# A Fourier mixing layer and a two-layer MLP in one kernel: the first MLP layer's blocks by seven products instead of eight

## The chip, the core and the metric

The kernel runs on one core of a Trainium2 chip. A core has a matrix engine (TensorE, PE in the profile; PEld is its load of the stationary operand), a vector engine (DVE), an activation engine (ACT), a general engine (POOL) and a queue for transfers (SP). Each engine works through its own list of instructions in order, and waits between engines are semaphores. Matmul results go to PSUM banks (tiles named `d`), from which ACT and DVE read them. The metric is the device time of a run in microseconds; lower is better.

## The reference

```python
h  = x + irfft2(rfft2(layernorm(x)) * (w_r + 1j * w_i))     # x: 2048 tokens x 576
h2 = h + relu(layernorm(h) @ w1) @ w2                        # w1: 576 x 4608, w2: 4608 x 576
```

All data is float32. The change concerns the last line only.

## The kernel before

The first part of the kernel computes the Fourier part by matmuls with constant tables. Then the normalised tokens lie transposed in four tiles `xc[c]` of 512 tokens each, and the MLP runs over 18 groups of 256 hidden units (`NG`), and in each group over the 4 token blocks. The sum over groups stays in `xs` (tile A) in SBUF.

**Three matmuls for a product.** TensorE is fed with the type float32r. To keep float32's precision, each operand is held as a high part `h` (ACT copies the value into float32r) and a low part `l` (the value minus `h`, on DVE or POOL); that pair of instructions is `split`. A product is then three matmuls: `h*h`, `h*l` and `l*h`.

**Layer 1.** `mm1` multiplies 128 hidden units by 512 tokens over a depth of 576: four tiles of 128 with three matmuls each, and a last tile of 64 that holds high and low side by side and takes two. That is 14 matmuls of 512 columns, and 28 for the 256 units of a step.

**Layer 2.** In groups 0 and 1 `mm2` does it plainly. From group 2 on (`WINO = 8`, the ninth step), the block of 256 units by 512 tokens and the block of `w2` are each cut into 2 by 2 parts, and the four part products come from seven products instead of eight (Winograd's form of Strassen's method): `prod` does one, with six matmuls of 288 columns, in one of two PSUM banks in turn. It needs sums and differences of the hidden parts (S1 to S4: POOL, then `split`) and of the weights (T1 to T4). After each product `add` (DVE, 128 x 576) adds the bank's present state to `xs`, and the next product but one goes into the same bank.

**The order.** Every engine's list is written by hand: it is the order of the calls in the code. `slot(i)` does layer 2 of step i while it does layer 1 of step i + 1, in four quarters: seven matmuls of layer 1, then two products of layer 2 with their adds, and between them the reading of the hidden block (`hid_a`: `relu_split` and a `Relu` copy), the splits and the next group's weights. The 64th slot, `slot_last`, has no layer 1 beside it and takes eight plain products.

Of the kernel before, what the change touches and what calls it, by code (L numbers as in the profile page):

```python
# [128 lines left out]
def kernel(ctx: ExitStack, tc: tile.TileContext, x, w_r, w_i, w1, w2, cc2, c1, fb, ib, c3, out):  # L129
    nc = tc.nc  # L130
    pool = ctx.enter_context(tc.tile_pool(name="sb", bufs=1))
    psum = ctx.enter_context(tc.tile_pool(name="ps", bufs=1, space=PSUM))

# [172 lines left out]
    def load_weights(g):  # L306
        v1, v2 = ebuf([128, 5, 256]), ebuf([128, 2, D])
# [4 lines left out]
        nc.sync.dma_start(v2, w2[f, :].rearrange("(a p) d -> p a d", p=128))  # L312
        raw[g] = (v1, v2)
# [4 lines left out]

    pieces = []

    def work(k):
        for _ in range(k):
            split(*pieces.pop(0))

    def split_weights(g, part):
# [6 lines left out]
        for k in range((5, 2)[part]) if g >= 2 else [slice(None)]:  # L332
            pieces.append((h[:, k], l[:, k], raw[g][part][:, k]))
        if g <= 2:
            work(len(pieces))
# [79 lines left out]
    xs = sb([128, NT, D], "A")  # L415
# [106 lines left out]
    hid = {}  # L522
    pend = {}

    def mm1(i, a, part=None):
        g, c = steps[i]
        w1h, w1l = wts[g, 0]
        if a == 0 and not part:
            pend[i] = None if i >= WINO else ps()
        p = hid_p(i, a) if i >= WINO else pend[i][:, 512 * a:512 * a + 512]  # L530
# [5 lines left out]
        for n_, (w, kt, xk) in enumerate(ops):  # L536
            if part is None or n_ // 7 == part:
                mm(p, w[:, kt, f], xc[c][:, xk, :], n_ == 0, n_ == len(ops) - 1)
        if i >= WINO:
            return  # L540
        if a == GF - 1:
            p = pend.pop(i).rearrange("p (a s) -> p a s", a=GF)
            hh, hl = sb([128, GF, 512], "D", 4, F32R), sb([128, GF, 512], "D", 4, F32R)
            nc.scalar.activation(hh, p, AF.Relu)  # L544
            nc.vector.scalar_tensor_tensor(hl, p, 0.0, hh, op0=ALU.max, op1=ALU.subtract)  # L545
            hid[i] = (hh, hl)

    seen = [0] * NC

    def mm2(i, tt):  # L550
# [12 lines left out]
        if tt == CH - 1:  # L563
            seen[c] += 1
            hid.pop(i)


    WINO = 8
    wps, fs = [], {}
    NAMES = ("B22", "T4", "B11", "B21", "T2", "T1", "T3")  # L570

    def wform(n):
        o = 6208 + 576 * NAMES.index(n)
        return tail[0][:, o:o + 288], tail[0][:, o + 288:o + 576]

    def wino_sums(g, *ns):
        v = raw[g][1]
        if 1 in ns:
            T = ebuf([128, 4, 288])
            fs["T1"], fs["T2"], fs["T3"], fs["T4"] = (T[:, i] for i in range(4))  # L580
            fs["B11"], fs["B12"], fs["B21"], fs["B22"] = v[:, 0, :288], v[:, 0, 288:], v[:, 1, :288], v[:, 1, 288:]
        for n_ in ns:
            o, a, b = (("T1", "B12", "B11"), ("T2", "B22", "T1"), ("T3", "B22", "B12"), ("T4", "B21", "T2"))[n_ - 1]
            nc.gpsimd.tensor_sub(fs[o], fs[a], fs[b])

    def wino_w(*names):
        for n in names:
            split(*wform(n), fs[n])

    def wino_tiles():  # L590
        D1, D2, D3 = (sb([128, 4, 256], "D", 4, F32R) for _ in range(3))
        E1, E2 = ebuf([128, 4, 256]), ebuf([128, 4, 256])
        hs = tail[0][:, 5184:5696], tail[0][:, 5696:6208]
        fs.update(p0=E1[:, 0:2], p1=E1[:, 2:4], S1=E2[:, 0], S2=E2[:, 1], S3=E2[:, 2], S4=E2[:, 3], S12=E2[:, 0:2])
        fs.update(A11=(D1[:, 0], D1[:, 1]), A12=(D1[:, 2], D1[:, 3]), A22=(D2[:, 0], D2[:, 1]), S4f=(D2[:, 2], D2[:, 3]))
        fs.update(S12f=(D3[:, 0:2], D3[:, 2:4]), S1f=(D3[:, 0], D3[:, 2]), S2f=(D3[:, 1], D3[:, 3]))
        fs.update(S3f=(tail[0][:, 5696:5952], tail[0][:, 5952:6208]))
# [6 lines left out]
    def hid_p(i, k):  # L604
        return wps[2 + k][:, 512 * (i % 2):512 * (i % 2) + 512]

    def hid_a(i, k):
        p = hid_p(i, k)
        if k == 0:
            relu_split(fs["A11"], p[:, :256])  # L610
            nc.scalar.activation(fs["p0"], p.rearrange("p (a n) -> p a n", a=2), AF.Relu)  # L611
            nc.gpsimd.tensor_sub(fs["S3"], fs["p0"][:, 0], fs["p0"][:, 1])  # L612
        else:
            relu_split(fs["A12"], p[:, :256])
            nc.scalar.activation(fs["p1"], p.rearrange("p (a n) -> p a n", a=2), AF.Relu)  # L615
            nc.gpsimd.tensor_add(fs["S1"], fs["p0"][:, 1], fs["p1"][:, 1])  # L616
            nc.gpsimd.tensor_sub(fs["S2"], fs["S1"], fs["p0"][:, 0])  # L617
            nc.gpsimd.tensor_sub(fs["S4"], fs["p1"][:, 0], fs["S2"])

    def prod(i, a, b, bank, first, end=True, whole=True):  # L620
        ah, al = fs[a]
        bh, bl = fs["B12f"] if b == "B12" else wform(b)
# [6 lines left out]
    def add(i, bank, *to):  # L629
        c = steps[i][1]  # L630
        P = wps[bank].rearrange("p (a n) -> p a n", a=2)[:, :, :288]
        for hs, hd in to:
            xt = xs[:, CH * c + 2 * hs:CH * c + 2 * hs + 2, 288 * hd:288 * hd + 288]
            nc.vector.tensor_add(xt, xt, P)  # L634
# [20 lines left out]
    def slot(i):  # L655
# [17 lines left out]
        if new:  # L673
            wino_w("T3", "B22")
# [140 lines left out]
```

## Time and profile before

| | |
|---|---|
| median of 3 runs | 1029.68 us (1028.57 to 1029.93) |
| profiled execution, first to last instruction (span) | 1026.5 us |
| median minus that span | 3.2 us |
| PE busy | 1011.1 us (98%) |
| PEld busy | 899.2 us (88%) |
| DVE busy | 741.4 us (72%) |
| ACT busy | 391.1 us (38%) |
| POOL busy | 326.0 us (32%) |
| mean granted clock of TensorE | 0.993 |
| steps 3 to 7, before the first slot | 200.4 to 264.1 us |
| slots | 264.1 to 1014.6 us |
| last block and the last stores | 1014.6 to 1026.5 us |

The profile gives no time of the profiled execution other than its span; the 3.2 us are what the runs' median has beside it. A row of the groups names the source line, the engine, the operation, the tiles written and read, their shape and count, and then the busy time, the mean duration of one, and the idle time of the engine just before them with what ended it. The means include the pipeline's length: neighbours on one engine can start before the one ahead has ended. Line 149 is the helper that issues the matmuls of layer 1 and of `mm2`, 627 the one of the seven products, 634 their adds, 317 the low part of a split, 152 ACT's copy, 584 and 612 to 618 POOL's sums.

### The profile page before, as it was taken

The page shows a single profiled execution, that of the slowest core. Times are in us where ns is not written, and L with a number is a line of the kernel's source. Part 1 is how long each engine was busy: PE and PEld are TensorE (multiplying, and loading weights), DVE is VectorE, ACT ScalarE, POOL GpSimd, SP SyncE. Part 2 cuts the span into 40 slices and gives each one's busy share as a digit, 9 for nine tenths or more (in the row PEclk, how much of TensorE's full clock was granted, in tenths as well). Part 3 has the DMA queues.
Part 4 walks back from the last instruction along what each step waited for, and adds up shares of the span by engine and source line. Part 5 has one row for each costly group of instructions (what it writes and reads, how often), then busy time and mean ns, then how long its engine had stood idle before and what let it go on. Part 6 is the DMA issues. An engine that isn't in the chain of part 4 may idle for free.

```text
span 1026.5 us, 17863 instructions
## 1 busy us (share of the span) xinstructions
PE 1011.1 (98%) x6894; PEld 899.2 (88%) x6894; DVE 741.4 (72%) x1366; ACT 391.1 (38%) x891; POOL 326.0 (32%) x429
## 2 busy tenths in 40 slices
PE   7999999999999999999999999999999999999997
PEld 6877678899999999999999999999999999999997
DVE  7689877334678777777777777877777777777774
ACT  5645354311233343343334343334334333334331
POOL 4201465110233333323232433333332323243321
PEclk7999999999999999999999999999999999999999
DMA  9944500110000000000110000000000011000024
GB/s 243 219 129 115 121 21 30 49 38 13 27 24 27 25 27 24 27 24 27 33 41 27 24 27 24 27 24 26 24 27 24 26 33 41 27 24 1 1 59 127
DMA packets 32101, 48.01 MB, mean 47 GB/s; under 512 B 2960, under 2 KB 22800, under 8 KB 32016
## 3 DMA queue, kind: packets, MB, share of 16 engines
q1 hardware_dynamic: 31280, 45.98, 16.7%
q8 instruction: 55, 0.90, 0.4%
q10 hardware_dynamic: 736, 0.89, 0.3%
q14 instruction: 30, 0.25, 0.1%
HBM read 42.13 MB, written 4.72 MB: 46 GB/s over the span
## 4 chain that ended last, share of the span: by engine, by line
PE 94%; DVE 3%; DMA 2%; SPq 0%; ACT 0%; issue 0%; DVEq 0%; ACTq 0%
PE d L149 58%; PE d L627 35%; DMA A<-in_A_x_dram 2%; DVE st L209 1%; PE d L509 1%; DMA X<-in_A_x_dram 0%; DVE A L469 0%; DVE D L545 0%; DVE e L253 0%; DVE mv L210 0%; ACT D L544 0%; DVE e L252 0%; DVE e L488 0%; SPq L424 0%; SPq L160 0%
## 5 line engine op out<-in xcount | busy, mean ns | idle before, releaser
L634 DVE TENSOR_TENSOR A<-A,d 128x576 f32<-128x576 f32 x445 | 332.5, 747 | 51.2 <-PE d L627 51.0
L627 PE MATMUL d<-X,D 128*128 128x288 f32 x2286 | 342.8, 294 | 0.0
L627 PEld LDWEIGHTS d<-X,D 128*128 128x128 f32 x2286 | 326.4, 188 | 14.7
L149 PE MATMUL d<-B,e 128*128 128x512 f32 x952 | 237.4, 390 | 0.0
L149 PEld LDWEIGHTS d<-B,e 128*128 128x128 f32 x952 | 171.9, 188 | 27.9 <-issue 0.2
L602 DVE SCALAR_TENSOR_TENSOR D<-d,D 128x256 fp32r<-128x256 f32 x191 | 81.1, 425 | 121.8 <-ACT D L601 121.8
L601 ACT ACTIVATE D<-d 128x256 fp32r<-128x256 f32 x191 | 73.0, 382 | 242.3 <-PE d L149 242.3
L616 POOL TENSOR_TENSOR e<-e 128x256 f32<-128x256 f32 x63 | 46.6, 740 | 350.0 <-ACT e L615 350.0
L149 PE MATMUL d<-C,e 128*128 128x512 f32 x476 | 119.0, 390 | 0.0
L149 PE MATMUL d<-X,e 128*128 128x512 f32 x476 | 118.8, 390 | 0.0
L152 ACT ACTIVATE X<-e 128x288 fp32r<-128x288 f32 (+2 forms) x176 | 69.8, 434 | 103.5 <-PE d L627 103.5
L317 DVE TENSOR_TENSOR D<-e,D 128x512 fp32r<-128x512 f32 x126 | 91.2, 724 | 19.5 <-ACT D L152 19.5
L612 POOL TENSOR_TENSOR e<-e 128x256 f32<-128x256 f32 x63 | 46.8, 744 | 170.1 <-ACT e L611 170.1
L149 PEld LDWEIGHTS d<-C,e 128*128 128x128 f32 x476 | 85.9, 188 | 13.8
L149 PEld LDWEIGHTS d<-X,e 128*128 128x128 f32 x476 | 85.9, 188 | 13.7
L152 ACT ACTIVATE D<-e 128x512 fp32r<-128x512 f32 x126 | 65.6, 521 | 73.7 <-POOL e L617 70.2
L317 DVE TENSOR_TENSOR X<-e,X 128x288 fp32r<-128x288 f32 (+2 forms) x176 | 82.8, 493 | 0.3 <-POOL r L212 0.3
L627 PEld LDWEIGHTS d<-X 128*128 128x128 f32 x378 | 57.2, 188 | 4.9
L627 PE MATMUL d<-X 128*128 128x288 f32 x378 | 60.4, 295 | 0.0
L149 PE MATMUL d<-e,D 128*128 128x288 f32 x384 | 52.7, 296 | 0.0
L149 PEld LDWEIGHTS d<-e,D 128*128 128x128 f32 x384 | 51.9, 189 | 0.7 <-ACT e L152 0.2
L617 POOL TENSOR_TENSOR e<-e,e 128x256 f32<-128x256 f32 x63 | 49.7, 790 | 4.9
(86 smaller groups left out, 938.0 us busy)
## 6 DMA issues: line engine op xcount, KB each, us to landing
e<-in_B_w_dram SPq DMA_DIRECT2D x18, 576.0 KB, 4.0
e<-in_B_w_dram SPq DMA_DIRECT2D x18, 512.0 KB, 3.7
A<-in_A_x_dram SPq DMA_DIRECT2D x16, 288.0 KB, 8.7
out_dram<-A SPq DMA_DIRECT2D x28, 144.0 KB, 2.5
X<-in_A_x_dram SPq DMA_DIRECT2D x12, 288.0 KB, 7.4
e<-in_B_w_dram SPq DMA_DIRECT2D x36, 64.0 KB, 3.5
B<-in_A_w_r_dram SPq DMA_DIRECT2D x15, 144.5 KB, 7.5
B<-in_A_w_i_dram SPq DMA_DIRECT2D x15, 144.5 KB, 7.1
```

Of the source, the lines that this page charges most:

```text
L149: nc.tensor.matmul(o, l, r, start=start, stop=stop)
L152: nc.scalar.activation(o, i, AF.Copy, **kw)
L209: nc.vector.bn_stats(st[:, i, h, :], xs[:, t0 + i, 288 * h:288 * h + 288])
L317: eng.tensor_sub(l, v, h)
L509: nc.tensor.transpose(pz[:, 128 * b:128 * b + 128], y[:, 128 * b:128 * b + 128], ident)
L601: nc.scalar.activation(h, p, AF.Relu)
L602: nc.vector.scalar_tensor_tensor(l, p, 0.0, h, op0=ALU.max, op1=ALU.subtract)
L612: nc.gpsimd.tensor_sub(fs["S3"], fs["p0"][:, 0], fs["p0"][:, 1])
L616: nc.gpsimd.tensor_add(fs["S1"], fs["p0"][:, 1], fs["p1"][:, 1])
L617: nc.gpsimd.tensor_sub(fs["S2"], fs["S1"], fs["p0"][:, 0])
L627: nc.tensor.matmul(P[:, tt], l[:, q], r, start=first and n_ == 0, stop=end and n_ == 2, skip_group_check=whole and not first)
L634: nc.vector.tensor_add(xt, xt, P)
```

## The change

From group 2 on, layer 1 is done by seven products too. Its block is 256 units by 1024 tokens, a *double*: two token blocks 2p and 2p + 1. The weights are cut into 2 by 2 parts of 128 units and a depth of 256, the tokens into parts of a depth of 256 and 512 tokens; the last 64 of the depth are added by two plain matmuls at four of the products. The sums of the token parts (T1 to T4, each with high and low part) are the same for every group. They are computed once, in steps 3 to 6 (`sum_jobs`), written to DRAM, and read back when p changes (`load_sum`): T1 and T2 over parts of `xc` that layer 1 no longer needs, T3 and T4 into a tile F. The order of the first eight steps has changed a little, and the scratch for software DMA is smaller.

A double's seven products go to three banks: a (which alternates between two places from double to double), b and c. Bank a collects products 0, 1, 3 and 6, and its state has to be read between them: `p1` after product 0, `u2` after 1, `c2` after 3. The two hidden blocks of the double, Z (second token block) and Y (first), arise from these states (`l1_post`, `l1_late`), with a sum of four POOL instructions for each (`hsum`, into one shared tile). `slot(d)` has seven rounds: in round r, product r of layer 1 of double d + 1, then products 2r and 2r + 1 of layer 2 of double d, then the reading for Y of double d (`l1_late`) and for double d + 1 (`l1_post`), then the weights. There are 31 such slots after the start, and a last one with 15 products of layer 2. Step 7 holds layer 1 of the first double.

```diff
-        for k in range((5, 2)[part]) if g >= 2 else [slice(None)]:
-            pieces.append((h[:, k], l[:, k], raw[g][part][:, k]))
...
+        split(h, l, raw[g][part])
...
+    steps = [(0, 0), (0, 1), (0, 2), (1, 1), (1, 0), (0, 3), (1, 3), (1, 2)]
...
+    def sum_jobs(p):
...
+        def tail_of(name, f, st):
+            h, l = (v3(v) for v in st)
+            jobs.append(lambda: act(h, f))
+            def low():
+                nc.vector.tensor_sub(l, f, h)
+                td[p, name] = d = dram.tile([128, 2, 1024], F32, name=f"t{p}{name}")
+                for k in range(2):
+                    nc.sync.dma_start(d[:, k], st[k].bitcast(F32))
+            jobs.append(low)
+        def diff(f, st, x, y):
+            w = v3(st[1].bitcast(F32))
+            jobs.append(lambda: (nc.gpsimd.tensor_sub(w, x[1], y[1]), nc.vector.tensor_sub(f, x[0], y[0])))
+            jobs.append(lambda: nc.vector.tensor_add(f, f, w))
...
+    def load_sum(p, n):
+        h, l = TF[n]
+        for k, o in enumerate((h, l)):
+            nc.sync.dma_start(o.bitcast(F32), td[p, n][:, k].rearrange("p (a n) -> p a n", a=2))
...
+    def l1_bank(d, n_):
+        k = {"a": d % 2, "b": 2, "c": 3}[n_]
+        return wps[2 + k // 2][:, 512 * (k % 2):512 * (k % 2) + 512]
+    def l1_prod(d, r):
...
+        bank, w, x, first, rest = (("a", "A11", "B11", 1, None), ("a", "S2", "T2", 0, None), ("c", "S1", "T1", 1, (1, 1)), ("a", "S3", "T3", 0, None),
+                                   ("b", "A12", "B21", 1, (0, 0)), ("c", "S4", "B22", 0, (2, 1)), ("a", "A22", "T4", 0, (1, 0)))[r]
+        o = l1_bank(d, bank)
+        (wh, wl), (xh, xl) = W1[w], X[x]
+        ops = [(a[:, k], b[:, k]) for k in range(2) for a, b in ((wh, xh), (wh, xl), (wl, xh))]
...
+    def hsum(p0, p1, o):
+        s1, s2, s3, s4 = (sums[:, 256 * k:256 * k + 256] for k in range(4))
+        nc.gpsimd.tensor_add(s1, p0[:, 256:], p1[:, 256:])
+        nc.gpsimd.tensor_sub(s2, s1, p0[:, :256])
+        nc.gpsimd.tensor_sub(s3, p0[:, :256], p0[:, 256:])
+        nc.gpsimd.tensor_sub(s4, p1[:, :256], s2)
+    def l1_post(d, r):
...
+        if r == 0:
+            act(p1, a)
+        elif r == 1:
+            act(u2, a)
+        elif r == 3:
+            act(c2, a)
+            nc.vector.tensor_add(c2, c2, c)
+            relu(c2, c2)
+            split(*Z["A2"], c2)
+        elif r == 4:
+            nc.vector.tensor_add(p1, p1, b)
+            relu(p1, p1)
+            if 0 < d < LAST:
+                split(*Y["A11"], p1[:, :256])
+        elif r == 5:
+            nc.vector.tensor_add(u2, u2, c)
+            relu(u2, u2)
+            hsum(u2, c2, None)
+            split(*Z["A11"], u2[:, :256])
+        elif r == 6:
+            split(*Z["S12"], sums[:, :512])
+            split(*Z["S34"], sums[:, 512:])
...
+    def l1_late(d, r):
...
+        if r == 0:
+            relu_split(Y["A2"], a)
+            if d < LAST:
+                relu(c2, a)
+                hsum(p1, c2, None)
+        elif d < LAST:
+            if r == 1:
+                split(*Y["S12"], sums[:, :512])
+            elif r == 2:
+                split(*Y["S34"], sums[:, 512:])
...
+    def weights(d, r):
...
+        if turn:
+            if r == 0 and g + 2 < NG:
+                load_w1(g + 2, vs[1])
...
+            if r == 6:
+                w2_split("T34", nc.vector)
+                w2_split("B22", nc.gpsimd)
+            for n_, k in (("T2", 1), ("T1", 2), ("T3", 3), ("T4", 6)):
+                if k == r:
+                    load_sum(doubles[d + 2][1], n_)
+        else:
...
+            if r == 5:
+                w1_split("S34", nc.gpsimd)
+            if r == 6:
+                for n_ in ("A2", "W4", "wd"):
+                    w1_split(n_, nc.gpsimd)
+    def slot(d):
+        for r in range(7):
+            l1_prod(d + 1, r)
+            for m in (2 * r, 2 * r + 1):
+                second(d, m)
+            l1_late(d, r)
+            l1_post(d + 1, r)
+            weights(d, r)
...
+        while jobs:
+            jobs.pop(0)()
+        w2_split("T34", nc.gpsimd)
+        w1_sums()
+        for n_ in ("A11", "S12", "S34", "A2", "W4", "wd"):
+            w1_split(n_, nc.gpsimd)
+        load_w1(FIRST + 1, vs[1])
...
+        for n_ in ("T2", "T1", "T3", "T4"):
+            load_sum(doubles[0][1], n_)
...
+        for r in range(7):
+            l1_prod(0, r)
+            if r % 2:
+                mm2(i, r // 2)
+            l1_post(0, r)
...
-    nc = _bacc.Bacc("TRN2", target_bir_lowering=False, num_devices=1)
+    nc = _bacc.Bacc("TRN2", target_bir_lowering=False, num_devices=1, dynamic_dma_scratch_size=512)
```

Where the instructions stand now, in the lists that the engines follow (line, operation, tile written and read, shape; the numbers behind the letters tell buffers apart).

ACT before, within two slots: L601 and L611 or L615 read a layer-1 bank `d`, D_2728 and X_2063 are high parts of S4 and S3, e_6684 of weights.

```order
L601 ACTIVATE D_2727<-d_2725 128x256
L611 ACTIVATE e_2730<-d_2725 128x512
L152 ACTIVATE D_2728<-e_2731 128x256
L152 ACTIVATE e_6684<-e_6474 128x256
L152 ACTIVATE X_2063<-e_2731 128x256
L601 ACTIVATE D_2727<-d_2726 128x256
L615 ACTIVATE e_2730<-d_2726 128x512
```

ACT now, from round 5 of a slot to round 0 of the next: L566 are relus (the first makes `u2`), A_1376 is `hsum`'s tile (D_2807 takes Z's S12, X_2065 behind it Z's S34), e_2659, e_2660 and cc take weights, D_2948 is Y's A2, and the last row copies bank a to `p1`.

```order
L566 ACTIVATE e_2802<-e_2802 128x512
L153 ACTIVATE X_2065<-e_2802 128x256
L153 ACTIVATE e_2659<-e_2549 128x512
L153 ACTIVATE D_2807<-A_1376 128x512
L153 ACTIVATE X_2065<-A_1376 128x512
L153 ACTIVATE e_2660<-e_2335 128x512
L153 ACTIVATE e_2660<-e_2335 128x256
L153 ACTIVATE cc_2661<-e_2549 128x128
L562 ACTIVATE D_2948<-d_2804 128x512
L566 ACTIVATE e_2803<-d_2804 128x512
L153 ACTIVATE e_2802<-d_2804 128x512
```

The bank's first reading now stands behind two rows that read POOL's sums, three weights and two readings of the double before.

DVE before, from the third quarter of a slot: L634 are the adds to `xs`, L602 reads a layer-1 bank for the low part, L317 are low parts of splits.

```order
L634 TENSOR_TENSOR A_1374<-A_1374,d_2834 128x2x288
L317 TENSOR_TENSOR X_2063<-e_2731,X_2063 128x256
L634 TENSOR_TENSOR A_1374<-A_1374,d_2835 128x2x288
L602 SCALAR_TENSOR_TENSOR D_2727<-d_2726,D_2727 128x256
L634 TENSOR_TENSOR A_1374<-A_1374,d_2834 128x2x288
```

DVE now, rounds 3 to 6: L747, L751 and L756 add a bank to `c2`, `p1` and `u2`, L323 behind each is the low part of the split of what ACT has made of it, L794 are the adds to `xs`.

```order
L747 TENSOR_TENSOR e_2803<-e_2803,d_2805 128x512
L323 TENSOR_TENSOR D_2806<-e_2803,D_2806 128x512
L794 TENSOR_TENSOR A_1376<-A_1376,d_2945 128x2x288
L794 TENSOR_TENSOR A_1376<-A_1376,d_2946 128x2x288
L751 TENSOR_TENSOR e_2803<-e_2803,d_2805 128x512
L323 TENSOR_TENSOR G_2662<-e_2803,e_2947 128x256
L794 TENSOR_TENSOR A_1376<-A_1376,d_2945 128x2x288
L794 TENSOR_TENSOR A_1376<-A_1376,d_2946 128x2x288
L756 TENSOR_TENSOR e_2802<-e_2802,d_2805 128x512
L323 TENSOR_TENSOR X_2065<-e_2802,X_2065 128x256
```

In each of three rounds an addition and a low part that follows from it, by way of ACT, now stand one behind the other, with the adds of the next round after them.

SP before, at the same place, loads a group's raw weights and nothing else:

```order
L309 DMA e_2330<-in_B_w_dram 128x4x256
L311 DMA e_2330<-in_B_w_dram 64x256 x2
L312 DMA e_2331<-in_B_w_dram 128x2x576
```

SP now, at the start of step 7 (t1T is a sum written to DRAM, t0T one that is read; e_2335 is the raw `w1`):

```order
L591 DMA t1T_2754<-e_2334 128x1024
L309 DMA e_2335<-in_B_w_dram 128x4x256
L311 DMA e_2335<-in_B_w_dram 64x256 x2
L615 DMA B_1393<-t0T_2442 128x1024 x2
L615 DMA X_2065<-t0T_2407 128x1024 x2
L615 DMA F_2793<-t0T_2511 128x1024 x2
```

The loads of the first sums stand behind the load of group 3's `w1` into the buffer of which group 2's is still being split.

More of the change, by code (lines that the diff above doesn't have):

```diff
@@ L726 @@
-    first = [(0, 0), (0, 1), (0, 2), (1, 0), (1, 1), (0, 3), (1, 2), (1, 3)]
-    steps = first + [(g, c) for g in range(2, NG) for c in range(NC)]
+        t, d = CH * c + 2 * hs, slice(288 * hd, 288 * hd + 288)
+        for k in range(2):
+            o = ov[k, :, t:t + 2, d]
+            o = bass.AP(tensor=o.tensor, offset=o.offset, ap=[list(o.ap[0]), [(1 + NT * (1 - 2 * k)) * D, 2], list(o.ap[-1])])
+            (nc.scalar if k and two else nc.sync).dma_start(o, xs[64 * k:64 * k + 64, t:t + 2, d])
@@ L795 @@
+        mm2(i, 3)
+    wps[:2] = ps(), ps()
+    hidden_bufs("Y")
+    split(*HF["Y"]["A11"], fx["p1"][0][:, :256])
+    for d in range(LAST):
+        slot(d)
+    slot_last(LAST)
 _INS = ["A_x", "A_w_r", "A_w_i", "B_w1", "B_w2"]
```

411 lines of the change are left out of this document (232 added, 179 removed).

## Prediction

> **What bounds the kernel now.** I read the page first, then the chain of waits, then a slot in the timeline, and the groups by shape for prices.
>
> ```profile
> span 1026.5 us, 17863 instructions
> PE 1011.1 (98%) x6894; PEld 899.2 (88%) x6894; DVE 741.4 (72%) x1366; ACT 391.1 (38%) x891; POOL 326.0 (32%) x429
> ```
>
> PE works all the time. In the chain of waits (start, length, what) the slots of the last 16 groups repeat exactly:
>
> ```profile
> 347.70 1.60 PE d L149 x7
> 359.62 1.60 PE d L149 x7
> ...
> 1002.93 1.60 PE d L149 x7
> 1014.05 7.16 PE d L627 x54
> ```
>
> A slot takes 11.92 us (359.62 − 347.70), and (1002.93 − 359.62) / 11.913 is 54 slots, so no slot is ever late. The timeline of one slot gives PE's prices:
>
> ```profile
> 565.16 1.75 PE L149 MATMUL d<-C,e 128*128 128x512 f32 x7
> 566.75 1.75 PE L627 MATMUL d<-X,D 128*128 128x288 f32 x12
> 568.33 0.85 PE L149 MATMUL d<-C,e 128*128 128x512 f32 x3
> ```
>
> From start to start, seven matmuls of 512 columns take 1.59 us (0.2275 each) and twelve of 288 take 1.58 (0.132 each). 28 × 0.2275 + 42 × 0.132 = 11.91: the slot is PE's own work and nothing else. Fewer matmuls shorten it, as long as nobody makes PE wait.
>
> **What the change takes from PE.** From group 2 on, layer 1 took 64 × 28 = 1792 matmuls of 512 columns. Now a double (256 units by 1024 tokens) takes seven products of 6 and four remainders of 2, that is 50, and 32 doubles take 1600. Layer 2 keeps its 2694 matmuls. 192 × 0.2275 = 43.7 us less work: the span would be 982.8, and a double 50 × 0.2275 + 84 × 0.132 = 22.45 us where two slots took 23.83. That is the floor, if PE never waits.
>
> **What it puts in PE's way.** The prices, by group and shape (count | busy, mean ns | idle before):
>
> ```profile
> L634 DVE TENSOR_TENSOR A<-A,d 128x576 f32<-128x576 f32 x445 | 332.5, 747 | 51.2 <-PE d L627 51.0
> L602 DVE SCALAR_TENSOR_TENSOR D<-d,D 128x256 fp32r<-128x256 f32 x191 | 81.1, 425 | 121.8 <-ACT D L601 121.8
> L545 DVE SCALAR_TENSOR_TENSOR D<-d,D 128x1024 fp32r<-128x1024 f32 x8 | 9.8, 1225 | 35.5 <-ACT D L544 35.5
> L317 DVE TENSOR_TENSOR D<-e,D 128x512 fp32r<-128x512 f32 x63 | 43.3, 687 | 0.2 <-ACT D L152 0.2
> L317 DVE TENSOR_TENSOR D<-e,D 128x256 fp32r<-128x256 f32 x63 | 47.9, 760 | 19.2 <-ACT D L152 19.2
> L317 DVE TENSOR_TENSOR X<-e,X 128x256 fp32r<-128x256 f32 x63 | 26.3, 418 | 0.0
> L152 ACT ACTIVATE D<-e 128x512 fp32r<-128x512 f32 x63 | 39.9, 633 | 73.7 <-POOL e L617 70.2 <-PE d L149 3.5
> L615 ACT ACTIVATE e<-d 128x512 f32<-128x512 f32 x63 | 37.8, 601 | 30.9 <-DVE D L602 30.9
> L152 ACT ACTIVATE X<-e 128x256 fp32r<-128x256 f32 x63 | 26.3, 418 | 103.5 <-PE d L627 103.5
> L616 POOL TENSOR_TENSOR e<-e 128x256 f32<-128x256 f32 x63 | 46.6, 740 | 350.0 <-ACT e L615 350.0
> L617 POOL TENSOR_TENSOR e<-e,e 128x256 f32<-128x256 f32 x63 | 49.7, 790 | 4.9
> L519 POOL TENSOR_TENSOR C<-e,C 128x512 fp32r<-128x512 f32 x4 | 5.1, 1298 | 3.4 <-ACT e L152 3.4
> ```
>
> and from the timeline the steps between neighbours and engines:
>
> ```profile
> 562.60 0.60 ACT L615 ACTIVATE e<-d 128x512 f32<-128x512 f32 x1 [0.49 <-DVE D L602]
> 563.28 0.73 POOL L616 TENSOR_TENSOR e<-e 128x256 f32<-128x256 f32 x1 [5.88 <-ACT e L615]
> 564.08 0.80 POOL L617 TENSOR_TENSOR e<-e,e 128x256 f32<-128x256 f32 x1
> 564.91 0.63 ACT L152 ACTIVATE D<-e 128x512 fp32r<-128x512 f32 x1 [1.14 <-POOL e L617]
> ...
> 571.93 0.75 DVE L634 TENSOR_TENSOR A<-A,d 128x576 f32<-128x576 f32 x1
> 572.59 0.42 DVE L317 TENSOR_TENSOR e<-e,e 128x256 fp32r<-128x256 f32 x1
> ```
>
> A neighbour on DVE starts 0.66 after an add of 0.75; a hand-over takes 0.03 (POOL to ACT, 564.88 to 564.91) to 0.08 us (ACT to POOL, 563.20 to 563.28).
>
> By volume no engine is full. Per double DVE does 14 adds (9.3), three adds of a PSUM block (0.70 each, between the 687 and 747 rows), one scalar_tensor_tensor of 512 (0.69, between its 256 and 1024 rows) and splits (some 4.6): 17 of 22.45 us. POOL does eight hidden sums (6.1) and its share of the weights (5920 columns per two doubles at the 740 and 1298 rows' 2.5 ns, some 8): 14. ACT does some 18 instructions of 512: 11.
>
> But the queues are in order, and the order rows of the section on the change show one closed loop. `l1_prod` of r = 1 adds into the PSUM bank that holds product 0, so PE first waits for `p1`, ACT's copy of it. On ACT that copy stands behind `relu(c2)`, behind Y's A2, behind the weights' splits and behind Z's S34, which waits for POOL's fourth `hsum`, which waits for `u2`. On DVE `u2` stands behind the splits and adds of r = 3 and r = 4, where DVE itself waits for ACT twice. Followed through one double, from PE's r = 1 to the next:
>
> - PE, r = 1 to the end of product 7: 20 × 0.2275 + 36 × 0.132 = 9.3, and 0.2 until its add starts.
> - DVE and ACT, r = 3: add 0.66, c2 0.70, its relu and split on ACT 2 × 0.63, low part 0.69, two adds 1.32: 4.6.
> - r = 4: p1 0.70, relu 0.63, split of 256 on ACT 0.42 and DVE 0.42, two adds 1.32: 3.5.
> - r = 5: u2 0.70, relu 0.63, four hsums at 0.76 (between 740 and 790), Z's S34 on ACT 0.63: 5.0.
> - boundary: S34's low part 0.69, two adds 1.32, Y's A2 0.69, relu and copy on ACT 1.1 (the second starts before the first has ended): 3.8. In every second double T34's low part stands there too, 0.67: 0.3 on the mean.
> - 13 hand-overs at 0.04: 0.5.
>
> Sum 27.2 us a double, where PE has work for 22.45: PE waits 4.75 us in each, at one place. From below: POOL at 0.74, hand-overs at 0.03 and every overlap of neighbours used, 26.2. From above: S34's low part runs while POOL splits the next W1. The 760 row against 418 shows that such a subtraction beside a POOL instruction lost 0.34 us; at most one POOL instruction of 512, 1.3 us: 28.5. I take 27.2, as most of its terms have their own row. 31 doubles × 4.75 = 147 us.
>
> **The clock.** PE has no long wait in the stretch above, but near the start it had. Timeline and windows (PE's busy us, ... , granted clock, DMA share, GB/s):
>
> ```profile
> 9.69 1.49 PE L149 MATMUL d<-cc,e 64*128 64x128 f32 x24 [2.52 <-DVE e L254]
> ...
> 20.62 5.66 PE L149 MATMUL d<-cc,e 64*128 64x128 f32 x57 [1.08 <-DVE e L254]
> ```
>
> ```profile
> 11.00:11.50 0.50, 0.19 (x10) 0.05 (x6) 0.50 (x3) 0.50 (x2) 0.42 (x2) 1.00 1.05 286
> 12.00:12.50 0.50, 0.50 (x8) 0.50 (x8) 0.40 (x3) 0.31 (x1) 0.16 (x1) 0.50 0.93 249
> 24.50:25.00 0.50, 0.50 (x6) 0.34 (x4) 0.50 (x2) 0.00 (x0) 0.40 (x2) 0.50 0.98 348
> 25.50:26.00 0.50, 0.50 (x9) 0.50 (x10) 0.50 (x3) 0.43 (x1) 0.00 (x0) 1.00 1.01 163
> ```
>
> After a wait of 2.52 us the granted clock was 0.50 at 12, some 4.5 us after the wait began, and it came back only after 4.6 us of work without a gap (20.62 to 25.2). A wait of 4.75 us in each double is longer. I price the drop at 4.6 us of half clock, 2.3 us lost, and all of it falls on the 9.3 us of PE at the loop's start: 31 × 2.3 = 71. Its ends are nothing and 4.65 (all 9.3 us at half clock); I take the 2.3, since PE works without a gap once the wait is over. The Trainium skill, "TensorE: Matmul & The Clock Gate", Part 1 on the HAM clock gate, asks for more: a whole idle window of some 3.4 us, free-running. By it, as an estimate, a wait of 4.75 us holds such a window in about four doubles of ten, at 1.7 us each, 21 us in all; here a wait of 2.52 us, shorter than that window, was followed by the drop, so the row decides.
>
> **The start.** Steps 3 to 6 now carry the token sums, and step 7 becomes the first double.
>
> ```profile
> 200.37:264.13 63.76, 63.76 (x382) 58.19 (x381) 23.99 (x36) 10.51 (x22) 6.12 (x8) 1.00 0.07 20
> L544 ACT ACTIVATE D<-d 128x1024 fp32r<-128x1024 f32 x8 | 8.2, 1026 | 56.9 <-PE d L149 56.9
> e<-in_B_w_dram SPq DMA_DIRECT2D x18, 512.0 KB, 3.7
> ```
>
> DVE was busy 24 of 64 us there. 24 new instructions of 1024 at 1.23 are 29 us, and eight waits for ACT's 1.03 some 8: in the 51 us of steps 3 to 6, that is 19 + 37 = 56, between 0 and 6 us too late. Then POOL must do T34, the sums of W1 and A11's split (1.4 + 3.4 + 0.7) before the first product, and A2 and W4's (4.6 more) before SP, whose queue has the next W1 load ahead, may issue the first sums' load: 1 MB, some 5 us after two loads of 3.7 that overlap. PE has little else then: some 15 us, and 5 more as T1, T3 and T4 come at 4.2 us each (250 GB/s) against products of some 3. I take 20, between 8 (DVE in time, POOL early) and 35. The other loads of sums cost nothing: each is issued some 20 us before its use, behind the product that read the old one, and 4.2 MB per 50 us is a third of what the rows above moved. Their writes (8.4 MB in 50 us) have the same cover. The smaller DMA scratch and the other order of the first eight steps add no instruction: nothing.
>
> **Sum.** 982.8 + 20 + 147 + 71 = 1221 us of span. The runs' median is 1029.7, 3.2 above the span of the profiled execution, so 1224.
>
> **Rivals.**
> - The clock holds (or falls seldom). For it: elsewhere gaps under 1 us did nothing, and the matmuls before 12 us were small. Then 1153; by the skill's rule 1174.
> - Faster: PE does not wait, since ACT's copy comes in time. DVE, ACT and POOL each have over 5 us of spare time per double, so it needs only that u2's chain ends 4.75 us earlier, say because DVE meets r = 3's and r = 4's splits done. It decides at 23.2 us a double, where 982.8 + 20 + 31 × 0.76 is the old span. With no wait in the loop: 1006, or 986 with a clean start too. Against it: the waits are true ones, and only spare time in the right place helps.
> - The sums come late from DRAM. A load that holds PE would add its 4.5 us once in two doubles, 16 × 4.5 = 72 on top: 1296. Against it: the 20 us of lead.
> - That the change does less than it says is out: the order has 50 such matmuls a double.
>
> **Chances.** Loop and clock 0.50; loop alone, or with some drops, 0.30; PE not held, faster, 0.10; late loads 0.03; worse than all this, with blocked subtractions and a longer half clock, 0.06; no change 0.01. The range goes from the loop's lower bound at full clock with a start of 8 (982.8 + 8 + 31 × 3.75 + 3.2 = 1110) to its upper bound of 28.5 with the drop and a start of 20 (982.8 + 20 + 31 × 8.35 + 3.2 = 1265). It leaves out the faster case, the late loads and the worst. A measurement of this kernel can tell 0.2% from no change, about 2 us. Slower 0.89, same 0.01, faster 0.10.
>
> **What would show it.** PE's busy share near 80%, and at the top of the waits PE at `l1_prod`'s line for ACT, about once a double, 4 to 5 us each, some 31 times; DVE and ACT with a large share of the chain of waits; a double of 29 to 30 us in the windows, or 27 with the clock at 1.00; digits under 9 in the clock's row; some 20 us without PE around 255 to 290. I am wrong if PE stays near 98%, if its waits are for DVE's adds or a DMA, or if the period is under 23.2.

## The result and the profile after

The changed kernel takes 1361.7 us (median; 1360.0 to 1364.0) against 1029.3: 1.323 times the time before, 95% interval 1.322 to 1.325. The prediction was 1224, with a range to 1265: the right side, but 138 us too low.

From the page of the changed kernel (busy us and share of the span, the clock that was granted in 40 slices, and the chain of work that ended last by engine):

```profile
span 1362.2 us, 17410 instructions
PE 1071.8 (79%) x6702; PEld 926.5 (68%) x6702; DVE 808.0 (59%) x1181; ACT 452.2 (33%) x836; POOL 548.4 (40%) x658
PEclk8999999789999999999989999988888988888989
PE 44%; DVE 21%; POOL 7%; ACT 6%; issue 4%; DMA 0%; DVEq 0%; SPq 0%; POOLq 0%
```

PE has 192 instructions less and falls from 98% to 79% busy. Every other engine has spare time, so something is serial. The list of PE's waits (who was waited for: us in all, times, longest) says where:

```profile
PE d L727 <- ACT e L153: 163.1, 32, 8.8
PE d L727 <- DVE e L747: 46.2, 32, 1.4
PE d L727 <- DVE e L751: 45.6, 32, 1.4
PE d L727 <- DMA B<-t0T: 9.5, 2, 8.8
```

The first row is the predicted wait of `l1_prod`'s r = 1 for ACT's copy of `p1`, once a double, some 5 us. The second and third were not predicted: 32 times 1.44 us behind DVE's add of `c2` (L747) and 32 times behind its add of `p1` (L751). The loads of sums hold PE at the start only.

The start of r = 1 in an early and a late double (timeline; in brackets the wait ahead):

```profile
375.60 1.65 PE L727 MATMUL d<-B,e 128*128 128x512 f32 x3 [5.75 <-ACT e L153]
1315.62 1.65 PE L727 MATMUL d<-B,e 128*128 128x512 f32 x3 [5.76 <-ACT e L153]
```

They are 28 doubles apart: (1315.62 − 375.60) / 28 = 33.57 us a double, where 29.5 was forecast and PE has 22.45 us of work. 31 × (33.57 − 22.45) = 345, and 982.8 + 345 leaves 34 us of the span for the start, where 20 was forecast. The forecast span was 1221, so 141 us of span are missing, and 126 of them, 31 × (33.57 − 29.5), are in the loop.

The chain of waits through one double (start, length, what; each piece released the next):

```profile
705.25 2.94 DVE X L323 x2
...
709.72 0.61 DVE D L563
...
710.35 0.60 ACT e L566
710.95 0.50 ACT e L153
...
711.49 2.93 PE d L727 x6
...
722.81 0.76 DVE A L794
723.57 0.61 DVE e L747
...
724.22 2.13 PE d L727 x8
...
728.74 0.61 DVE e L751
...
729.39 2.11 PE d L727 x8
...
739.00 1.54 DVE X L323
```

It is the loop of the prediction: low parts, adds, relu and copy at the boundary, then PE, then the rounds 3 to 5, then POOL's sums. Two things in it are new. At 724.22 and 729.39 the chain goes through PE, which starts the products of r = 4 and r = 5 0.04 us after a DVE add has ended; the prediction had PE free there and went by ACT's relu and split. And at the boundary S34's and T34's low parts take 2.94 us together. The groups by shape (count | busy, mean ns) show that a low part has no one price:

```profile
L323 DVE TENSOR_TENSOR X<-A,X 128x512 fp32r<-128x512 f32 x32 | 49.5, 1548 | 4.8 <-ACT X L153 2.3
L323 DVE TENSOR_TENSOR e<-A,e 128x512 fp32r<-128x512 f32 x31 | 21.2, 685 | 0.0
L323 DVE TENSOR_TENSOR X<-e,X 128x576 fp32r<-128x576 f32 x15 | 20.1, 1340 | 0.0
```

The first is Z's S34, 1548 ns; the second is Y's S34, the same shape and kind, 685 ns. The first runs while POOL splits weights; in the double above (timeline):

```profile
704.52 3.06 POOL L323 TENSOR_TENSOR X<-e,X 128x576 fp32r<-128x576 f32 x2
...
705.25 1.68 DVE L323 TENSOR_TENSOR X<-A,X 128x512 fp32r<-128x512 f32 x1
```

Last, the clock behind two of the waits for the copy (windows: PE's busy us, ..., granted clock, DMA share, GB/s):

```profile
711.49:714.21 2.72, 2.72 (x6) 2.15 (x7) 0.00 (x0) 0.63 (x1) 2.36 (x4) 0.50 0.00 0
714.21:716.20 1.99, 1.99 (x14) 1.98 (x12) 0.59 (x1) 1.43 (x3) 0.71 (x2) 0.78 0.00 0
...
746.57:749.36 2.79, 2.79 (x14) 2.79 (x13) 0.75 (x1) 1.12 (x2) 2.71 (x4) 0.52 0.44 120
749.36:752.79 3.43, 3.43 (x22) 3.08 (x21) 1.95 (x3) 0.00 (x0) 0.08 (x1) 1.00 0.78 282
```

The six matmuls of r = 1 and the twelve behind them take 4.71 us (711.49 to 716.20) and, a double later, 5.52 (743.84 to 749.36), instead of 1.37 + 1.58 = 2.95: 1.8 and 2.6 us lost. In all 31 slots the six matmuls of r = 1 took 2.79 to 2.93 us, as at 711.49, where they take 1.65 at full clock.

### The profile page after: what moved, and what is told of

Same layout as the page of the kernel before. It is cut to its first block, busy times and chain, and to the rows that moved or that the text cites. A ratio compares the mean times of both kernels' runs of the same rounds, so it can differ in the third digit from the quotient of the medians.

```text
span 1362.2 us, 17410 instructions
## 1 busy us (share of the span) xinstructions
PE 1071.8 (79%) x6702; PEld 926.5 (68%) x6702; DVE 808.0 (59%) x1181; ACT 452.2 (33%) x836; POOL 548.4 (40%) x658
## 4 chain that ended last, share of the span: by engine, by line
PE 44%; DVE 21%; POOL 7%; ACT 6%; issue 4%; DMA 0%; DVEq 0%; SPq 0%; POOLq 0%
PE d L727 24%; PE d L789 19%; DVE A L794 10%; DVE X L323 5%; ACT e L566 3%; POOL A L732 2%; POOL A L731 2%; POOL A L734 2%; ACT X L153 2%; DVE D L563 1%; DVE e L751 1%; DVE e L747 1%; DVE e L756 1%; ACT e L153 1%; DMA B<-t0T 0%
## 5 line engine op out<-in xcount | busy, mean ns | idle before, releaser
L794 DVE TENSOR_TENSOR A<-A,d 128x576 f32<-128x576 f32 x445 | 332.1, 752 | 331.1 <-PE d L789 319.9
L789 PE MATMUL d<-X,D 128*128 128x288 f32 x1548 | 264.8, 319 | 3.6 <-DVE D L563 2.0
L789 PEld LDWEIGHTS d<-X,D 128*128 128x128 f32 x1548 | 254.9, 214 | 18.0 <-DVE D L563 2.2
L153 ACT ACTIVATE e<-d 128x512 f32<-128x512 f32 (+2 forms) x144 | 85.0, 590 | 290.4 <-PE d L727 245.0
L323 POOL TENSOR_TENSOR X<-e,X 128x576 fp32r<-128x576 f32 (+1 forms) x49 | 74.4, 1532 | 239.1 <-ACT X L153 239.1
L566 ACT ACTIVATE e<-e 128x512 f32<-128x512 f32 x96 | 60.7, 632 | 312.1 <-DVE e L756 123.9
L323 POOL TENSOR_TENSOR e<-e,e 128x256 fp32r<-128x256 f32 (+2 forms) x65 | 86.7, 1344 | 123.6 <-ACT e L153 123.6
L727 PE MATMUL d<-F,e 128*128 128x512 f32 x384 | 99.4, 394 | 0.0
L789 PE MATMUL d<-X,e 128*128 128x288 f32 x496 | 84.7, 295 | 0.0
L727 PEld LDWEIGHTS d<-F,e 128*128 128x128 f32 x384 | 68.8, 188 | 11.3
L323 DVE TENSOR_TENSOR D<-A,D 128x512 fp32r<-128x512 f32 x63 | 66.8, 1060 | 1.3 <-ACT D L153 1.3
L323 DVE TENSOR_TENSOR X<-e,X 128x256 fp32r<-128x256 f32 (+2 forms) x48 | 41.5, 864 | 37.1 <-ACT X L153 36.7
```

What stands on the lines that cost most here:

```text
L153: nc.scalar.activation(o, i, AF.Copy, **kw)
L323: eng.tensor_sub(l, v, h)
L566: nc.scalar.activation(o, i, AF.Relu)
L727: nc.tensor.matmul(o, a, b, start=bool(first) and n_ == 0, stop=n_ == len(ops) - 1, skip_group_check=not first)
L789: nc.tensor.matmul(P[:, tt], l[:, q], r, start=first and n_ == 0, stop=end and n_ == 2, skip_group_check=whole and not first)
```

## The experiments

All times are medians, and ratios are against the kernel before on the same chip (1028.6 to 1028.8 us there, so that times from different chips can be compared). Each of the first five kernels is the changed kernel with one edit.

**ACT's copy first.**

```
+            if r:
+                l1_late(d, r)
             l1_post(d + 1, r)
+            if r == 0:
+                l1_late(d, r)
```

> The only edit: in round 0 of a double, ACT's copy of p1 is issued ahead of the last double's late work (the relu with the low part of Y's A2, and relu(c2)) and no longer behind it. Theory 1, ACT's queue order makes the loop: the copy then waits only for Z's S34 (high part) and the weights' splits, so S34's low part (1.6 us), half of T34's (0.7), two adds (1.5), A2's low part (0.7) and the relu (0.5) leave the loop and 0.7 us of weights' splits stay in it. PE's wait at r = 1 falls from 5.06 us to under 1, the granted clock stays at 1.00 there, which gives another 2.2 us: 33.57 - 4.3 - 2.2 = 27.1 us a double, 1362 - 31 x 6.5 = 1160 us (1130 to 1190). Theory 2, DVE is the bound at the boundary and the copy is only where PE happens to meet it: PE's wait moves to DVE's adds a few products later, the clock drops there, and the time stays above 1300.

Measured: 1343.4 us, ratio 1.306 (1.304 to 1.308). Theory 2's number, but not its reason. Its list of waits and its timeline:

```profile
PE d L727 <- ACT e L566: 139.3, 31, 5.3
```

```profile
729.75 0.57 ACT L153 ACTIVATE e<-d 128x512 f32<-128x512 f32 x1
...
732.55 0.60 ACT L566 ACTIVATE e<-d 128x512 f32<-128x512 f32 x1 [1.74 <-DVE D L563]
733.20 0.93 PEld L727 LDWEIGHTS d<-B,e 128*128 128x128 f32 x3 [4.10 <-ACT e L566]
```

The copy ends at 730.32, but PE starts at 733.20, behind `relu(c2)` (L566). That relu reads bank a of the *last* double, and r = 1 writes bank a of the next one: different banks, but halves of one PSUM tile. It is not DVE's adds that PE meets, but the same thing as at r = 4 and r = 5, where b and c are the two halves of a tile.

**Other banks.**

```
-        k = {"a": d % 2, "b": 2, "c": 3}[n_]
+        k = {"a": 2 * (d % 2), "b": 1, "c": 3}[n_]
```

> The only edit: the three PSUM banks of layer 1 are dealt out so that b and c no longer stand in one PSUM tile (a in the first half of either tile, b and c in the second halves). Theory 1, the two PE waits of 1.44 us behind DVE's adds of c2 and p1 (r = 4 and r = 5) come from that shared tile, not from data: both go, PE runs ahead of DVE, and as DVE then has an add, a low part and two adds to do in any case, 1.0 to 1.44 us is won each time: 1362 - 31 x (2.0 to 2.9) = 1272 to 1300 us. Theory 2, DVE's own queue holds r = 4 and r = 5: the waits go from PE's list, but the wait for ACT's copy at r = 1 grows by as much, and the time stays within 15 us of 1362.

Measured: 1295.8 us, ratio 1.260 (1.258 to 1.262), theory 1. Both rows of 1.44 us are gone; left are

```profile
PE d L727 <- ACT e L153: 151.0, 32, 8.8
PE d L727 <- DVE e L756: 35.5, 16, 2.3
```

66 us less, though a new row has come: in odd doubles a now shares its tile with c, and r = 6 waits for the add of `u2` (L756). The program's dependencies hold a matmul back for a reader of the other half of its tile. The Trainium skill, "PSUM — Partial Sum Buffer", section "PSUM bank collisions raise a hardware error", speaks of collisions within one bank only, and a half of this tile, 512 fp32 columns, is a bank there; so by that page these waits guard against no collision. No run here shows PE writing one half of such a tile while another engine reads the other, as the program never lets them.

**The weights' splits moved off the boundary.**

```
+            if r == 5:
+                weights(d, r)
             l1_post(d + 1, r)
+            if r == 0 and d:
+                weights(d - 1, 6)
+            if r < 5:
+                weights(d, r)
```

> The only edit: the weights' splits of round 5 are issued ahead of that round's post work, and those of round 6 (T34 on DVE, and B22, A2, W4 and wd on POOL) behind round 0 of the next double; T4's load follows. Theory 1, DVE's low parts with two SBUF inputs lose their time to POOL's splits beside them: Z's S34 low part falls from 1.55 to 0.7 us, and T34's (1.34 in every second double) leaves the loop: 1.5 us a double, 1362 - 31 x 1.5 = 1315 us (1295 to 1330). Theory 2, such a low part is as slow without POOL: only T34 is won, 0.67 us a double, 1341 us.

Measured: 1307.3 us, ratio 1.271 (1.269 to 1.273): 54 us less, theory 1. The two low parts, by group:

```profile
L323 DVE TENSOR_TENSOR X<-A,X 128x512 fp32r<-128x512 f32 x32 | 22.2, 694 | 4.8 <-ACT X L153 2.0
L323 DVE TENSOR_TENSOR X<-e,X 128x576 fp32r<-128x576 f32 x15 | 17.0, 1134 | 25.9 <-ACT X L153 25.9
```

S34's low part falls from 1548 to 694 ns; the instruction is the same, and what POOL does beside it is not. The Trainium skill, "SBUF — State Buffer", section "SBUF: two separate sides", calls the port pair that DVE and POOL share an exclusive lock, taken for a whole instruction by a DVE operation with two SBUF inputs against a POOL operation that reads SBUF. The trace agrees as far as it goes: the added time, 0.85 us, is less than one POOL subtraction of 512 (1.3 us), as if DVE waited for the rest of the one that runs.

**PE kept busy in the wait.**

```
+            if r == 1:
+                for _ in range(18):
+                    nc.tensor.matmul(l1_bank(0, "b"), W1["A11"][0][:, 0], khalf(0, 0)[0][:, 0], ...)
             l1_prod(d + 1, r)
```

> The only edit: ahead of l1_prod's r = 1 stand 18 more matmuls of 512 columns into bank b, which nobody reads; at 0.2275 us they take 4.1 us of the 4.4 to 5.8 us in which PE waits. Theory 1, the wait costs its own length and 2.2 us of half clock behind it: with PE busy the granted clock stays at 1.00 at r = 1, its product takes 1.55 us, not 2.93, and the time falls by 31 x 2.2 = 68 us to 1294. Theory 2, the half clock costs nothing, as DVE and ACT are late in that stretch anyway: the clock shows 1.00 and the time stays within 15 us of 1362. Theory 3, the gap that is left or the end of the wait itself still brings the clock down: no change in either.

Measured: 1297.2 us, ratio 1.261 (1.259 to 1.263): 64.5 us less by doing more, theory 1. Windows of the 18 extra matmuls and of r = 1 behind them:

```profile
711.91:716.17 4.26, 4.26 (x20) 3.19 (x18) 3.26 (x4) 2.02 (x6) 3.70 (x5) 1.00 0.13 31
716.45:717.94 1.49, 1.49 (x7) 1.23 (x7) 0.00 (x0) 0.38 (x1) 1.41 (x3) 1.00 0.85 277
```

The mean granted clock of the run rises from 0.914 to 0.984. 64.5 / 31 = 2.1 us a double is what the half clock costs, and the gap of 0.27 us that is left ahead of r = 1 does not bring it down.

**The first loads ahead.**

```
-        load_w1(FIRST + 1, vs[1])
...
             load_sum(doubles[0][1], n_)
+        load_w1(FIRST + 1, vs[1])
```

> The only edit: in the last step before the doubles, the loads of the first token sums are issued ahead of the load of the next W1. Theory 1, at the start the sums' load stands on SP behind that load, which waits for POOL's splits of A2, W4 and wd: T2's load begins at the end of DVE's sums (262) instead of 272.7, PE's wait of 8.7 us for it goes, and as PE's next waits are for POOL and ACT, 4 to 9 us are won: 1353 to 1358. Theory 2, POOL's and ACT's own late work at the start holds the first products anyway: under 2 us.

Measured: 1352.7 us, ratio 1.315 (1.313 to 1.316): 9 us less, the upper end of theory 1. In the changed kernel SP's queue had held T2's load from 262 to 272.7.

**Copy and banks together.**

> Both edits together: p1's copy ahead of the last double's late work, and banks b and c (and the two a) in different PSUM tiles. In the copy-first run alone PE's r = 1 waited, though the copy had been done for 2.9 us, for relu(c2), which reads the other half of the PSUM tile that r = 1 writes. Theory 1, the shared tile alone held PE there: now r = 1 waits for the copy only, that is for S34's high part and the weights' splits, the wait falls from 4.4 us to under 1 and the half clock (2.2 us) goes too: 1296 - 31 x (4 to 6.5) = 1094 to 1172. Theory 2, DVE's boundary work (two low parts, two adds, A2's low part, 6.4 us without a gap) is the bound: PE's wait moves to DVE's adds, and the time stays above 1230.

Measured: 1202.3 us, ratio 1.169 (1.167 to 1.170). Apart, the two edits won 18 and 66 us, together 159. So the shared tile was what held r = 1 once the copy came early: r = 1 now waits 1.46 us in one double (at 695.95) and not at all in the next (at 729.52). The time stays 30 us above theory 1's interval all the same, because PE waits at two other places in every second double, where this dealing puts c beside a:

```profile
703.04 2.93 PE L727 MATMUL d<-X,e 128*128 128x512 f32 x6 [2.93 <-ACT e L153]
...
721.46 2.10 PE L727 MATMUL d<-F,e 128*128 128x512 f32 x6 [2.26 <-DVE e L756]
```

The first is r = 2, which writes c and waits for ACT's copy of `u2` out of a. The second is r = 6, which writes a and waits for the add that reads c. Windows behind these two waits:

```profile
703.04:706.83 3.79, 3.79 (x9) 3.02 (x10) 0.72 (x1) 0.84 (x2) 3.55 (x6) 0.50 0.02 4
721.46:724.42 2.96, 2.96 (x9) 2.37 (x10) 0.61 (x1) 2.18 (x4) 2.20 (x4) 0.67 0.00 0
```

Such a wait does not bring the clock down every time. Of the 15 products r = 2 that stood behind 2.93 us, 7 ran at half clock throughout, 4 partly, and 4 at full clock (at 362.05 the six matmuls took 1.65 us).

**All four edits, and another dealing of the banks.** The second kernel differs from the first by one line, which puts b beside a of its own double and c into the other tile:

```
-        k = {"a": 2 * (d % 2), "b": 1, "c": 3}[n_]
+        k = {"a": 2 * (d % 2), "b": 2 * (d % 2) + 1, "c": 3 - 2 * (d % 2)}[n_]
```

> All four edits: p1's copy first, the other banks, the weights' splits of rounds 5 and 6 moved off the boundary, the first sums' loads ahead on SP. If the parts add up (18 + 66 + 54 + some 5 us from 1362, and 31 x 4 to 6.5 more where copy and banks together free r = 1), 1018 to 1095. Theory 1, the loop no longer holds PE but for the odd doubles' r = 6, which shares its tile with the bank that u2's add reads (2.3 us in 16 doubles): 982.8 + 25 of start + 16 x 2.3 + 3 = 1048. Theory 2, the serial chain relu, split, add of rounds 3 to 5 still ends last: 25 to 26 us a double, 1090 to 1120.

> As the kernel with all four edits, but b always shares its PSUM tile with a of the same double, and c stands in the other tile. Theory 1, the odd doubles' wait of r = 6 for u2's add goes (2.3 us in 16 doubles, with the chain behind it): 20 to 40 us less than with the other dealing. Theory 2, c's first product (r = 2) now waits in every double for the last double's A2 and relu(c2), which read its tile: the same time or up to 30 us more.

Measured: 1216.3 us (ratio 1.183, 1.180 to 1.185) and 1155.6 us (1.123, 1.122 to 1.124). The first misses both theories: it is slower than copy and banks alone. The moved splits had got into the way at their new place, as the second kernel's waits show:

```profile
PE d L727 <- POOL G L323: 52.1, 15, 3.5
PE d L727 <- ACT e L153: 26.3, 32, 8.8
PE d L789 <- POOL X L323: 19.1, 15, 1.3
```

W4's low part (G) and B22's (X) stand on POOL behind the late `hsum`s and are needed in round 2; in the first kernel PE waited 43.6 us for W4's. The other dealing of the banks is worth 61 us, more than the 20 to 40 expected. The expectation counted the wait of r = 6 only (35.5 us in the first kernel, now gone); that of r = 2 for the copy of `u2` went with it, and PE's waits for ACT's copies fell from 63.3 to 26.3 us.

**The loop as the prediction priced it.** The last dealing and the moved splits, with the copy in its old place:

> The changed kernel with two edits: b always in the PSUM tile of its own double's a, c in the other (no wait of PE on the tile's other half at r = 4 and 5), and the weights' splits of rounds 5 and 6 moved off the boundary (no low part of DVE beside a POOL subtraction). p1's copy stays behind the late work. This is the loop as the prediction walked and priced it, without T34 in it (27.2 - 0.3 us) and with the half clock (2.2): Theory 1, the two things left out are all that the prediction missed in the loop: 29.1 us a double, 982.8 + 34 of start + 31 x (29.1 - 22.45) + 3 = 1226 us (1205 to 1245). Theory 2, more was missed, or the two overlap: over 1260, or under 1190.

Measured: 1220.1 us, ratio 1.186 (1.185 to 1.188), theory 1. (1218.0 − 982.8 − 34) / 31 + 22.45 = 28.9 us a double. Part of its chain of waits, where one double goes as the prediction walked it, from `c2`'s add by relu and split to the next adds, without PE:

```profile
753.00 0.61 DVE e L747
753.63 0.64 ACT e L566
754.29 0.64 ACT D L153
...
756.97 0.61 DVE e L751
...
759.34 2.83 POOL X L323 x2
```

The last row holds the low parts of B1 and T12 (T12's split is one of those that were moved), which in every second double stand ahead of `hsum`. In the other double the chain runs through PE's products as far as round 5, without a wait. So the agreement is of the size, not of every step.

**What is left taken away.** On top of the kernel with the last dealing: W4, wd and B22 split on POOL ahead of the late `hsum`s, A2 and T34 behind them, and Z's S34 behind the copy. At the start, the splits of A11 and T34 and the sums of W1 go ahead of the last token sums.

```
+            if r == 0:
+                if d:
+                    split(*HF["Z"]["S34"], sums[:, 512:])
+                    weights(d - 1, 6)
+                l1_late(d, r)
```

> From the parity kernel (span 1154.1), whose list of waits has PE 15 times behind POOL's low part of W4 (52.1 us), 15 times behind POOL's low part of B22 (19.1 us) and 31 times behind ACT's copy of p1 (17.5 us, which stands behind S34's high part): W4, wd and B22 are now split on POOL ahead of the late hsums, A2 and T34 behind them, and Z's S34 behind p1's copy; at the start A11's split, T34 and W1's sums are issued ahead of the last token sums. Theory 1, these waits were the last in the loop: 52 + 19 + 17 us go, and 5 to 10 of the 14 us in which PE waits at the start: 1155.5 - 88 - 7 = 1060 us (1030 to 1075). Theory 2, the time of the loop is set by POOL and DVE behind them: other waits take their place, over 1100.

Measured: 1045.8 us, ratio 1.017 (1.016 to 1.018), theory 1. A small wait is left, 30 times:

```profile
720.52 0.68 DVE L563 SCALAR_TENSOR_TENSOR D<-d,D 128x512 fp32r<-128x512 f32 x1
721.24 0.60 ACT L566 ACTIVATE e<-d 128x512 f32<-128x512 f32 x1 [1.83 <-DVE D L563]
...
721.89 0.50 PE L727 MATMUL d<-X,e 128*128 128x512 f32 x1 [0.34 <-ACT e L566]
```

Here c stands beside the last double's a. Its product waits for `relu(c2)`, and that, itself a reader of the bank, for another reader of it, the low part of A2 on DVE (L563). The next kernel turns these two round, and at the start issues A11's, T34's and S12's splits and the first two loads within the step before:

```
-            relu_split(Y["A2"], a)
+            relu(Y["A2"][0], a)
             if d < LAST:
                 relu(c2, a)
+            nc.vector.scalar_tensor_tensor(Y["A2"][1], a, 0.0, Y["A2"][0], op0=ALU.max, op1=ALU.subtract)
+            if d < LAST:
                 hsum(p1, c2, None)
```

> From the last kernel (span 1043.6): relu(c2) is issued on ACT ahead of A2's low part on DVE, which reads the same PSUM bank and held it back, and at the start A11's, T34's and S12's splits and the loads of T2 and T1 are issued within the last step that still carries token sums, ahead of T4's sum. Theory 1, PE's 30 waits for relu(c2) at r = 2 go with the slow start behind them (some 0.5 us a double, 15 us), and at the start PE's waits of 8.2 and 4.3 us go, but the wait for T3's load takes part of them back (some 9 us are won): 1045.8 - 15 - 9 = 1022 us (1014 to 1032), 0.7% under the kernel before. Theory 2, the start is held by DVE's token sums, whatever stands ahead of them, and the loop by other short waits: 1035 to 1046.

Measured: 1026.4 us, ratio 0.998 (0.997 to 0.999): now under the kernel before. The half on the loop held: r = 1 of two neighbouring doubles,

```profile
708.55 1.55 PE L727 MATMUL d<-B,e 128*128 128x512 f32 x6
731.41 1.55 PE L727 MATMUL d<-B,e 128*128 128x512 f32 x6
```

are 22.86 us apart, and no wait of PE in the loop is left in the list. The half on the start failed: PE's second wait there grew to 12.2 us, for the first copy of `p1`. ACT had done its splits at 263.0 and then waited again:

```profile
270.57 0.60 ACT L153 ACTIVATE e<-d 128x512 f32<-128x512 f32 x1 [7.55 <-DMA t1T<-e]
```

By this row the copy waited for a buffer of tile e, out of which a token sum was still being stored; in SP's list the loads of T2 and T1 now stood ahead of that store. So the splits on ACT, which the next expectation names, were the smaller part of the wait. The last kernel puts POOL's share of T3 ahead of A11's and T34's splits, S12's split behind T3's low part, and the two loads earlier (245 instead of 258):

> From the last kernel (1026.4 us), whose first double begins late: POOL's splits of A11 and T34 stand there ahead of its share of the sum T3, which DVE waits 5.7 us for, and the first p1 copy stands 12.2 us behind splits on ACT. Now that share of T3 comes first on POOL, then A11, T34 and W1's sums, and S12's split behind T3's low part. Theory 1, PE's r = 0 starts at 253 and not 256, the copy of p1 comes after T4's high part at some 259, r = 1 starts at 260 and not 271, and then T3's load (267) holds r = 3, so that some 8 us are won: 1018 us (1013 to 1023). Theory 2, ACT's copy stays behind splits that wait for POOL: 1024 to 1029.

Measured: 1018.7 us, ratio 0.991 (0.989 to 0.992), theory 1, though r = 1 starts at 262.9 and not at 260. ACT's wait for the store is 1.2 us now. Which of the moves shortened it was not tested.

```profile
span 1016.3 us, 17442 instructions
PE 984.5 (97%) x6702; PEld 863.8 (85%) x6702; DVE 771.9 (76%) x1181; ACT 448.6 (44%) x836; POOL 566.6 (56%) x658
```

The same instructions for the products as in the changed kernel, in another order and with the banks dealt differently, make it 0.9% faster than the kernel before, not 32% slower.

## Why the prediction was right and wrong

**PE's own work: right.** 22.86 us a double without waits against the floor of 22.45, and 97% busy at a span of 1016.3.

**The wait for ACT's copy: right in place, cause and size.** 4.75 us once a double was forecast; the timeline has 5.75 and 4.37 in turn, 5.06 on the mean. That the loop makes it, and not volume, is shown by the last kernels, in which the same work leaves no such wait.

**The clock: right.** 2.3 us a double and 71 us in all were forecast, 64.5 us came back when PE was kept busy. The other reading that the prediction gave, by the Trainium skill's "TensorE: Matmul & The Clock Gate", Part 1, an estimate of 21 us in all for waits of which four in ten hold a whole idle window, is out: all 31 waits for the copy were followed by slow matmuls, and so were some of the shorter ones in the experiments. One bound was wrong without effect: 9.3 us of PE's work done at half clock lose 9.3 us, not the 4.65 that the prediction gave as the upper end; its range went by 2.3.

**The loop's sum: wrong, 4.1 us a double too short.** This is the step that failed: "Sum 27.2 us a double, where PE has work for 22.45: PE waits 4.75 us in each, at one place." By legs, the chain of two neighbouring doubles gives, on the mean, where the forecast (with the half clock, and the hand-overs put to the leg of the rounds) had

| leg | forecast | measured |
|---|---|---|
| PE, r = 1 to the end of product 7 | 11.8 | 11.3 and 12.1: 11.7 |
| rounds 3 to 5, to S34's low part | 13.6 | 16.2 and 16.2: 16.2 |
| boundary, to the next r = 1 | 4.1 | 4.8 and 6.2: 5.5 |

Two terms were mis-sized.

- Rounds 3 to 5, +2.6 us. PE was taken to run ahead while DVE and ACT finish r = 3 and r = 4. It can't: b and c lie in one PSUM tile, and the product of r = 4 waits for `c2`'s add, that of r = 5 for `p1`'s. Both waits could be seen beforehand: the rows of DVE's order in the section on the change name the same tile, d_2805, in L747 and L751. Dealing the banks out anew won 66 us in the one way, and 61 more in the other (in the kernel with all four edits).
- The boundary, +1.4 us. The low part of S34 was priced at 0.69, the price without a neighbour, and T34's likewise. Beside POOL's splits they take 1.55 and 1.34, T34's in every second double, which is 1.2 of the 1.4. The prediction had the row for it (760 against 418 ns) and used it only for its upper bound, and only once. Moving the splits won 54 us.

With both mended the time was 1220, where the prediction's walk, with the start as measured, gives 1226.

**The start: too short by 14 us.** 34 for 20. PE's first wait, 8.8 us, is for A11's high part, which on ACT stands behind T4's and so behind DVE's last token sums; the prediction had DVE 0 to 6 us late. SP's order, which its 20 contained, was worth 9 us when it was turned round. What makes up the rest was not taken apart. The 3.2 us that the prediction put between span and time were 1.8 in the profiled execution (1364.0 against 1362.2).

**Sums late from DRAM: rightly set aside.** PE waits for no load after the start.

**The range: too narrow above.** Its upper end took one blocked subtraction a double as the worst and had no term for waits of the tiles. The rival "PE not held" decides as it said: it took a loop under 23.2 us a double to be faster, and the kernels at 22.86 are.

## What to carry to other kernels

In a loop through several engines, write down for every matmul which tile it writes and who else still reads any part of that tile: two banks in one PSUM tile were one thing to this program's dependencies, and which banks share a tile was worth more here than the matmuls saved. Price an instruction by the row that has its neighbour, not by the row of its shape alone. When a chain has several causes, an edit to one can be worth little until another is made too (18 and 66 us apart, 159 together).

## What the runs showed of the hardware that was not expected

In the changed kernel the clock fell behind each of PE's 31 waits for the copy (2.6 to 5.8 us) and behind none of its 63 waits of 1.44 us (the six matmuls of r = 5 took 1.63 to 1.66 us each time). Waits in between went either way: of 15 waits of 2.93 us in the kernel with copy and banks, 11 were followed by a drop and 4 were not, and the 2.96 us behind one of 2.26 us were granted 0.67 on the mean. 18 idle matmuls, 4.26 us of work that is thrown away, made the kernel 64.5 us faster. The same subtraction of 512 columns took DVE 1548 or 694 ns, as POOL had splits beside it or not.
